# Half products for the last 384 columns of a dense layer, and its activation moved into the next layer

## The chip, the cores and the metric

The program runs on one core of one Trainium2 chip. Its time is device microseconds (us) for one execution; the kernel before is given as the median of 3 executions, and one more execution was recorded by the hardware profiler.

## The reference

```python
x = attention(rmsnorm(q), rmsnorm(k), v)          # 4 batches, 12 heads, 448 tokens, 64 each
x = x.transpose(0, 2, 1, 3).reshape(1792, 768)
# each token goes to one of 8 experts, 224 tokens per expert
out[mask] = np.maximum(x[mask] @ w1[e], 0) @ w2[e]   # w1 768x1024, w2 1024x768
h = out @ w_in                                     # dense layer 1: 768 -> 2048
g = np.where(h > 0, h, np.exp(np.minimum(h, 0)) - 1)   # ELU
return g @ w_out                                   # dense layer 2: 2048 -> 768
```

Inputs and results are float32.

## The kernel before, in words

Every float32 operand of a matmul is split into two float16 tiles (high and low part), and a product takes three matmuls: high x high, high x low, low x high. ScalarE writes the high part, VectorE the low part (`scalar_tensor_tensor`).

Attention and routing come first, then eight experts `e`: `first(e, f)` multiplies into a hidden slice, `second(e, d)` gives 128 of the 768 outputs for the expert's 224 tokens, and `result(e, d, ps)` splits them into `xc`. The tile `xc[0]` holds tokens (columns of the matmul) 0 to 511, `xc[1]` the remaining 384 of a half; the tokens are taken as two rows of 896, index `h`, so that dense layer 1 is a 2x2 block product: input halves of 384 features by token halves of 896 (blocks A), output halves of 1024 by input halves of 384 (blocks B).

Such a 2x2 product can be made of seven half products in place of eight (`winograd`). It needs sums of the operand blocks: S1 = A21+A22, S2 = S1-A11, S3 = A11-A21, S4 = A12-S2, and T1 to T4 in the same way from the weights. In `combine(c, d)` (L964) GpSimd makes S1 to S4 of dense layer 1, for each of the four 128-token chunks `c` of the 512 columns, in three steps `d`; the calls stand between `first` and `second` of experts 2 to 5. `wi_prep(f)` makes weight blocks and T1 to T4 of step `f`: words decoded and split by VectorE and ScalarE.

Dense layer 1 has eight steps `f`, each for two times 128 outputs. In a step, `fewer` (L1173) takes the 512 columns by seven half products of 9 matmuls, and `plain` (L1160) takes the 384 columns by four sums of 18 matmuls, one after each of four half products. Each result goes through `elu` (L1151): Exp and Relu on ScalarE, one `scalar_tensor_tensor` on VectorE, and a store to DRAM `g_d`. Beside it `wi_prep(f + 1)` and `wo_prep(k)`, which prepares layer 2's weights, run on VectorE and ScalarE; the T1 to T4 of layer 2 go to DRAM `t_d`.

Dense layer 2 (L1223 to L1269) has seven groups `g` of two times 128 tokens. `operands(g)` loads the four blocks from `g_d` (tiles `q`), makes their sums on VectorE and splits all seven; `layer2(g, a)` runs seven half products of 24 matmuls of 384 columns into PSUM sums `o_a`, `o_b`, `o_c` and scatters the result. Before group 0, `load_t` (L1100) brings layer 2's T3 and T1 into the tile `ex` (which takes the place of `sums`) and T4 into part of `xc[0]`, 1536 KB each; T2 comes by parts into `t2`.

The order on each engine is the order in the code, apart from the parts where the tile framework places instructions by its own simulated times (the dense layers and `wi_prep`); `issue_after` holds an instruction behind another one. DMAs of these parts are issued by the SP queue.

Of the kernel before, what the change touches and what calls it, by code (L numbers as in the profile page):

```python
# [21 lines left out]
P = 128  # L22
# [761 lines left out]
class Weights:  # L784
# [28 lines left out]
    def fetch(self, pool, w2_d):  # L813

        f = pool.tile([P, 7168], F32, name="b", tag="ex", bufs=1)
# [41 lines left out]
PS = ("a", 2), ("b", 3), ("c", 3)  # L857
A11, A12, S2, S3, S1, S4, A22 = range(7)
# [3 lines left out]
def winograd(pp, name, n, product, snap, add, copy):  # L862

    a, b, c = (pp.tile([P, 512], F32, name=name + t, tag=t, bufs=k)[:, 0:n] for t, k in PS)
    product(b, A11, B11, True)
    p1 = snap(b)
    product(a, A12, B21, True)
    add(a, p1, 0, 0)
    product(b, S2, T2, False)
    u2 = snap(b)  # L870
    product(c, S3, T3, True)
    p7 = snap(c)
    product(b, S1, T1, False)
    add(b, p7, 1, 1)
    product(c, A22, T4, False)
    add(c, u2, 1, 0)
    product(b, S4, B22, False)
    return copy(b, 0, 1)
# [15 lines left out]
def moe(tc, xp, homes, xs, idx, idh, W, rows, ring, w1_d, w2_d, wi_d, wo_d, lin, g_d, t_d, out):  # L894
    nc = tc.nc
    with tc.tile_pool(name="mp", bufs=1, space=PSUM, reuse_waits="tile") as pp:
# [7 lines left out]
        wic, sums, kept = {}, [], []  # L904
# [23 lines left out]
        with tc.tile_pool(name="m1", bufs=1, reuse_waits="tile") as sp:  # L928
# [35 lines left out]
            def combine(c, d):  # L964
                if not sums:
                    x = homes.tile([P, 14336], F16, name="sums", tag="ex", bufs=1)
                    sums.append(x[:, 0:12288].rearrange("p (k d j c) -> p k d j c", k=4, d=3, j=2))
                    kept.extend(x.bitcast(F32)[:, c:c + 512] for c in (6144, 6656))
                x, y = slice(c * P, c * P + P), xc[0]
                s, uv = (z.rearrange("p (k c) -> p k c", k=4) for z in kept)  # L970
                s1, s3, s2, s4 = (s[:, k] for k in range(4))
                u, v = uv[:, 0:2], uv[:, 2:4]
                add = lambda o, p, q, op=ALU.add: nc.gpsimd.tensor_tensor(o, p, q, op)  # L973
                add(u, y[:, 1, d, :, x], y[:, 1, d + 3, :, x])
                add(v, y[:, 0, d, :, x], y[:, 1, d, :, x], ALU.subtract)
                add(s[:, 2:4], y[:, 0, d:d + 4:3, 0, x], y[:, 0, d:d + 4:3, 1, x])
                add(s[:, 0:2], uv[:, 0:4:2], uv[:, 1:4:2])
                add(s2, s1, s2, ALU.subtract)
                add(s4, s4, s2, ALU.subtract)
                hi, lo = (sums[0][:, :, d, j, x] for j in range(2))  # L980
                nc.gpsimd.tensor_copy(hi, s)
                add(lo, s, hi, ALU.subtract)
# [39 lines left out]
            with tc.manual_schedule():  # L1022
# [17 lines left out]
                for e in range(E):  # L1040
# [23 lines left out]
                    for d in range(3 * (1 < e < 6)):  # L1064
                        combine(e - 2, d)
# [9 lines left out]
                    xe[e + 1] = x  # L1075
            wi_prep(0)
            for d in range(6):
                second(E - 1, d, ws[2, E - 1, d])
        with tc.tile_pool(name="wb", bufs=1, reuse_waits="tile") as wp:
# [25 lines left out]
            def operands(g, late=None):  # L1105
# [13 lines left out]
                todo, ahead = [], elus[-1].ins if late else None  # L1119
                held = lambda n: tc.issue_after(ahead) if late and n else ExitStack()  # L1120
                for n, (f, (a11, a12, a21, a22)) in enumerate(parts):
                    s1, s2, s3, s4 = [x[:, f] for x in s]
# [14 lines left out]
                if late:  # L1137
                    for n, k in enumerate((A11, A12, A22, S2)):
                        with held(n > 1):
                            split(k, (ex[:, 12288:14336] if n == 0 else flat[0][:, 2048 * n - 2048:2048 * n]).rearrange("p (f h c) -> p f h c", f=8, h=2))  # L1140
# [7 lines left out]
            elus = []  # L1148

            with tc.tile_pool(name="l1", bufs=1, side="right", reuse_waits="tile") as sp:  # L1150
                def elu(f, cb, k, ps, done=False):  # L1151
                    c0, c1 = CB[cb]
                    h, r = k % 2, k // 2
                    e = sp.tile([P, 512], F32, tag="e", name=f"e{f}_{cb}{h}{r}", bufs=5)[:, 0:c1 - c0]
# [4 lines left out]
                    return e, nc.sync.dma_start(g_d[g, k, :, f].rearrange("g p c -> p g c"), e.rearrange("p (g c) -> p g c", c=P))  # L1159

                def plain(f):
                    n = CB[1][1] - CB[1][0]
                    for h, r in ((0, 0), (0, 1), (1, 0), (1, 1)):
                        t, bufs = PS[2 - r]
                        ps = pp.tile([P, 512], F32, name=f"l{f}_1{h}{r}", tag=t, bufs=bufs)[:, 0:n]
                        w = wic[f + 8 * r]
                        for d in range(6):
                            for m, (i, j) in enumerate(((0, 0), (0, 1), (1, 0))):
                                nc.tensor.matmul(ps, w[:, i, d * P:(d + 1) * P], xc[1][:, h, d, j], start=d == 0 and m == 0, stop=d == 5 and m == 2)  # L1169
                        yield elu(f, 1, 2 * r + h, ps)[1]  # L1170

                def fewer(f, beside):
                    made = {}  # L1173
                    x = {A11: xc[0][:, 0, 0:3], A12: xc[0][:, 0, 3:6], A22: xc[0][:, 1, 3:6]} | dict(zip((S1, S3, S2, S4), (sums[0][:, k] for k in range(4))))
                    w = {B11: (f, 0), B21: (f, 384), B22: (f + 8, 384), T1: ((f, 1), 0), T2: ((f, 1), 384), T3: ((f, 3), 0), T4: ((f, 3), 384)}

                    def product(ps, p, q, first):
                        k, c = w[q]
                        for d in range(3):
                            for m, (i, j) in enumerate(((0, 0), (0, 1), (1, 0))):  # L1180
                                nc.tensor.matmul(ps, wic[k][:, i, c + d * P:c + d * P + P], x[p][:, d, j], start=first and d == 0 and m == 0,  # L1181
                                                 stop=d == 2 and m == 2, skip_group_check=True)
                        if p in (A11, S2, S3, A22):
                            next(beside)

                    homes = [*kept, sp.tile([P, 512], F32, tag="e", name=f"z{f}", bufs=5)]
# [12 lines left out]

                    winograd(pp, f"l{f}_", 512, product, snap, add, copy)  # L1200
                    return made

                for f in range(8):
# [19 lines left out]
            with tc.tile_pool(name="l2a", bufs=1, side="right", reuse_waits="tile") as sa, \  # L1223
# [8 lines left out]
                def layer2(g, a):  # L1232
# [21 lines left out]
                    winograd(pp, f"o{g}_", 384, product, snap, add, copy)  # L1254
# [3 lines left out]
                for g in range(7):  # L1258
                    ops = (first, then, operands(g))[min(g, 2)]
                    if g > 1:  # L1260
                        with tc.issue_after(last.ins):
                            next(ops)
                    elif g:
                        next(ops)
                    else:
                        wt[T4] = load_t(T4, flat[0][:, 6144:12288])
                    behind = lambda k: tc.issue_after(elus[-2].ins if g == 0 else snaps[1 if k in (A11, A12) else 2].ins) if g < 2 else ExitStack()
# [42 lines left out]
```

## Time and profile before

| | |
|---|---|
| median of 3 executions | 942.63 us (940.82 to 944.12) |
| the profiled execution | 941.17 us |
| its span | 939.4 us, mean granted TensorE clock 0.995 |
| PE busy | 918.9 us, 98% of the span |
| DVE busy | 763.2 us, 81% |
| ACT busy | 582.6 us, 62% |
| POOL busy | 370.8 us, 39% |

PE is TensorE's matmuls, PEld its weight loads, DVE VectorE, ACT ScalarE, POOL GpSimd, SP the queue that issues DMAs. The span is what the profiler saw from the first to the last instruction; 941.17 us is the same execution's time, 1.8 us longer. Busy shares are over the whole span, which has stages with different limits: attention and routing to about 290 us, the experts to 540 us, dense layer 1 to 742 us, dense layer 2 to the end. Engine instructions overlap slightly at their ends, so the distance between two starts, not the listed duration, tells what one costs in a busy stretch.

### The profile page before, as it was taken

How to read it: one execution, taken by the hardware profiler on the slowest of the kernel's cores; microseconds unless marked ns; L12 is line 12 of the kernel's file. 1: busy time of each engine (PE TensorE's matmuls, PEld its weight loads, DVE VectorE, ACT ScalarE, POOL GpSimd, SP SyncE). 2: the span in 40 equal slices, each digit the busy share in tenths (PEclk: the TensorE clock that was granted, in tenths of full speed). 3: DMA queues.
4: the chain of work that ended last, by engine and by line, in shares of the span. 5: the costliest groups of instructions: out<-in, count | busy, mean ns of one | idle time of the engine just before them, and what ended most of it. 6: DMA issues, size and time to landing. Idle time of an engine off the chain costs nothing.

```text
span 939.4 us, 18782 instructions
## 1 busy us (share of the span) xinstructions
PE 918.9 (98%) x6855; PEld 614.0 (65%) x6855; DVE 763.2 (81%) x1455; ACT 582.6 (62%) x1251; POOL 370.8 (39%) x552
## 2 busy tenths in 40 slices
PE   7999999999998999999999999999999999999997
PEld 3555555555544899999999955555555566666664
DVE  8999998899868877998888899999999776655430
ACT  7989999999864655566655466666666643333320
POOL 5779999999622200699997000000000001000000
PEclk9999999999998999999999999999999999999999
DMA  9644444453235956887867257777776974232000
GB/s 351 211 111 151 122 141 123 147 165 83 66 83 194 240 185 216 240 228 233 269 218 224 94 187 221 238 226 236 235 230 196 360 265 146 85 105 97 35 35 33
DMA packets 100353, 164.93 MB, mean 176 GB/s; under 512 B 32672, under 2 KB 65952, under 8 KB 99872
## 3 DMA queue, kind: packets, MB, share of 16 engines
q1 hardware_dynamic: 96048, 152.66, 51.9%
q0 software_dynamic: 2400, 11.01, 3.5%
q8 instruction: 55, 0.90, 0.4%
q14 instruction: 42, 0.34, 0.1%
q10 hardware_dynamic: 1808, 0.01, 0.1%
HBM read 131.66 MB, written 31.99 MB: 174 GB/s over the span
## 4 chain that ended last, share of the span: by engine, by line
PE 87%; DVE 6%; POOL 2%; ACT 1%; DMA 1%; issue 1%; POOLq 0%; DVEq 0%; ACTq 0%
PE ph L989 12%; PE py L997 12%; PE o_b L1240 11%; PE l L1169 10%; PE o L320 7%; PE l_b L1181 7%; PE o_c L1240 6%; PE s L243 5%; PE pt L296 4%; PE l_c L1181 3%; PE o_a L1240 3%; PE l_a L1181 2%; DVE s L248 1%; PE xt L948 1%; PE pt L294 1%
## 5 line engine op out<-in xcount | busy, mean ns | idle before, releaser
L1256 POOL DMA_INDIRECT out<-xc,id x14 | 14.6, 1046 | 410.1 <-issue 261.8
L1240 PEld LDWEIGHTS <-a 128*128 128x128 f16 x1080 | 105.7, 98 | 69.8
L1014 DVE SCALAR_TENSOR_TENSOR w<-fw,w 128x768 f16<-128x768 f32 (+1 forms) x90 | 109.3, 1224 | 8.6 <-ACT w L1011 8.4
L997 PE MATMUL py<-h,w 128*128 128x224 f16 x1152 | 114.2, 259 | 0.0
L997 PEld LDWEIGHTS <-w 128*128 128x128 f16 x1152 | 109.8, 98 | 0.2
L248 DVE TENSOR_REDUCE s<-s 128x1 f32<-128x448 f32 x168 | 104.8, 626 | 5.4 <-PE s L243 4.8
L267 ACT ACTIVATE p<-s,nb,r 128x448 f32<-128x448 f32 x144 | 104.4, 726 | 4.1 <-DVE nb L254 3.0
L1169 PE MATMUL l<-xc,wic 128*128 128x384 f16 x576 | 100.3, 326 | 0.0
L989 PE MATMUL ph<-xe,w 128*128 128x224 f16 x1008 | 97.7, 259 | 0.0
L989 PEld LDWEIGHTS <-w 128*128 128x128 f16 x1008 | 96.6, 98 | 0.0
L305 ACT ACTIVATE e<-pt 128x448 f32<-128x448 f32 (+2 forms) x208 | 80.9, 429 | 14.5 <-PE pt L296 14.2
L320 PE MATMUL o<-e,v 128*64 128x448 f32 x384 | 87.8, 558 | 0.0
L1011 ACT ACTIVATE w<-fw 128x768 f16<-128x768 f32 (+1 forms) x90 | 81.7, 921 | 5.7 <-DMA fw<-w 5.7
L1169 PEld LDWEIGHTS <-wic 128*128 128x128 f16 x576 | 56.4, 98 | 41.6
L296 PE MATMUL pt<-idn,p 128*128 128x128 f32 x432 | 70.9, 276 | 0.9 <-ACT p L267 0.9
L296 PEld LDWEIGHTS pt<-idn,p 128*128 128x128 f32 x432 | 50.0, 141 | 23.9 <-ACT e L305 12.3
L1134 DVE SCALAR_TENSOR_TENSOR a<-s,a 128x1024 f16<-128x1024 f32 (+2 forms) x30 | 33.1, 1116 | 33.7 <-ACT a L1133 33.7
L973 POOL TENSOR_TENSOR sums<-sums 128x128 f32<-128x128 f32 (+2 forms) x48 | 58.0, 1208 | 2.8
L243 PE MATMUL s<-ks,qh 128*128 128x448 f16 x144 | 51.2, 355 | 1.9 <-ACT p L267 1.0
L1240 PE MATMUL o_b<-wb,a 128*128 128x384 f16 x312 | 52.0, 326 | 0.0
L243 PE MATMUL s<-ks,ql 128*128 128x448 f16 x144 | 50.7, 352 | 0.0
L961 ACT ACTIVATE xc<-py 128x224 f16<-128x224 f32 (+2 forms) x54 | 18.1, 335 | 51.0 <-PE py L997 46.5
(340 smaller groups left out, 1957.2 us busy)
## 6 DMA issues: line engine op xcount, KB each, us to landing
fw<-w SPq DMA_DIRECT2D x54, 384.0 KB, 3.8
fw<-w SPq DMA_DIRECT2D x36, 512.0 KB, 4.6
xwi<-wi SPq DMA_DIRECT2D x16, 768.0 KB, 7.2
xwo<-wo SPq DMA_DIRECT2D x16, 768.0 KB, 5.1
q<-g_d SPq DMA_DIRECT2D x24, 512.0 KB, 3.7
qT<-qT SPq DMA_DIRECT2D x24, 448.0 KB, 4.2
qk<-qk SPq DMA_DIRECT2D x23, 448.0 KB, 3.5
g_d<-e SPq DMA_DIRECT2D x32, 256.0 KB, 3.7
```

The source lines that it names most:

```text
L243: nc.tensor.matmul(ps[:, 0:448], q[:, o:o + P], ks[:, 448 * h:448 * h + 448], start=n == 0, stop=n == 1)
L248: nc.vector.tensor_reduce(d["s", u][:, 448:449], d["s", u][:, 0:448], AX.X, ALU.max, negate=True)
L267: nc.scalar.activation(dst, d["s", u][:, 0:448], AF.Exp, bias=d["nb", u], scale=d["r"][:, rc:rc + 1], accum_out=d["sm"][:, rc:rc + 1])
L296: nc.tensor.transpose(pt[:, j * P:(j + 1) * P], p[j][:, h, 64 * h + c * P:64 * h + (c + 1) * P], idn)
L320: nc.tensor.matmul(d["o"][64 * h:64 * h + 64, 0:448], d["v"][:, c + 4 * h, :], d["e", min(2 * c + h, 6)], start=c == 0, stop=c == 3)
L989: nc.tensor.matmul(ps, w[:, i, d * P:(d + 1) * P], x[:, d, j], start=d == 0 and n == 0, stop=d == 5 and n == 2)
L997: nc.tensor.matmul(ps, w[:, i, f * P:(f + 1) * P], h[:, f, j], start=f == 0 and n == 0, stop=f == 7 and n == 2)
L1011: nc.scalar.activation(ws[k][:, 0], fs[k], AF.Copy, scale=SW)
L1014: nc.vector.scalar_tensor_tensor(ws[k][:, 1], fs[k], SW, ws[k][:, 0], ALU.mult, ALU.subtract)
L1169: nc.tensor.matmul(ps, w[:, i, d * P:(d + 1) * P], xc[1][:, h, d, j], start=d == 0 and m == 0, stop=d == 5 and m == 2)
L1181: nc.tensor.matmul(ps, wic[k][:, i, c + d * P:c + d * P + P], x[p][:, d, j], start=first and d == 0 and m == 0, stop=d == 2 and m == 2, sk ...
L1240: nc.tensor.matmul(ps, a[x][:, f, i], wt[b][f][:, j], start=first and f == 0 and k == 0, stop=f == 7 and k == 2, skip_group_check=True)
```

## The change

The 384 columns are taken by seven half products as well. The seven products of the two halves alternate (`winograd` is now a generator and yields after each product), with the PSUM tags `b` and `c` exchanged for the third sum. The operand sums of the 384 columns are made by `combine(c)`, c = 4 to 6, and each call now does a whole 128-token chunk in 16 instructions; six of the seven calls run on GpSimd, the last on VectorE. S1 is written over A21 in `xc`; the tile `sums` grows to 19200 float16 and holds the other sums of both halves and a scratch part. Dense layer 1 no longer applies ELU: it scales, adds and stores. ELU is applied in `operands(g)` of layer 2. Layer 2's T3 and T1 now go into parts of the same tile `sums`, T1 behind the last product, and T4 is issued ahead of them.

```diff
+            def combine(c):
...
+                t, eng = c > 3, nc.vector if c == 6 else nc.gpsimd
+                a11, a12, a21, a22 = q = [s[:, k:k + 3] for k in (0, 3, 6, 9)]
+                for k, z in enumerate(q):
+                    add(z, y[:, 3 * k:3 * k + 3, 0, x], y[:, 3 * k:3 * k + 3, 1, x])
+                add(a22, a21, a22)
+                add(a21, a11, a21, ALU.subtract)
+                add(a11, a22, a11, ALU.subtract)
+                add(a12, a12, a11, ALU.subtract)
+                for o, z in zip((y[:, 6:9], sums[t][:, 0:3], sums[t][:, 3:6], sums[t][:, 6:9]), (a22, a11, a12, a21)):
+                    eng.tensor_copy(o[:, :, 0, x], z)
+                    add(o[:, :, 1, x], z, o[:, :, 0, x], ALU.subtract)
...
-                    for d in range(3 * (1 < e < 6)):
-                        combine(e - 2, d)
+                    if e > 1:
+                        combine(e - 2)
...
+            combine(5)
             wi_prep(0)
             for d in range(6):
                 second(E - 1, d, ws[2, E - 1, d])
+            combine(6)
...
+                        for o, z, x in zip(y, t, raw):      # in operands(g)
+                            nc.scalar.activation(z, x, AF.Exp)
+                            nc.scalar.activation(z, z, AF.Relu, bias=1.0, scale=-1.0)
+                            nc.vector.scalar_tensor_tensor(o, x, -1.0, z, ALU.mult, ALU.min)
...
-                    nc.scalar.activation(e, ps, AF.Exp, scale=1.0 if done else CH2)
-                    nc.scalar.activation(e, e, AF.Relu, bias=1.0, scale=-1.0)
-                    elus.append(nc.vector.scalar_tensor_tensor(e, ps, -1.0 if done else -CH2, e, ALU.mult, ALU.min))
+                    return e, nc.scalar.activation(e, ps, AF.Copy, scale=CH2)
...
-                    late = fewer(f, plain(f) if f < 7 else repeat(None))
-                ex = homes.tile([P, 14336], F16, name="ex", tag="ex", bufs=1)
+                    late = {}
+                    both = fewer(f, 0, late), fewer(f, 1, {})
+                    for k in (0, 0, 1, 0, 1, 0, 0, 1, 0, 1, 0, 1, 1, 1) if f == 0 else (0, 1) * 7 if f < 7 else (0,) * 7:
+                        next(both[k])
+                ex = whole[0]
                 first = operands(0, late)
                 next(first)
-                wt = {T3: load_t(T3, ex[:, 0:6144]), T1: load_t(T1, ex[:, 6144:12288])}
+                wt = {T3: load_t(T3, ex[:, 0:6144]), T4: load_t(T4, flat[0][:, 6144:12288])}
                 then = operands(1)
-                for last in plain(7):
-                    next(then)
+                for k, _ in enumerate(both[1]):
+                    if k in (1, 4, 5, 6):
+                        next(then)
+                wt[T1] = load_t(T1, ex[:, 8192:14336])
...
-    nc = bacc.Bacc("TRN2", target_bir_lowering=False, num_devices=1)
+    nc = bacc.Bacc("TRN2", target_bir_lowering=False, num_devices=1, dynamic_dma_scratch_size=8192)
```

The next two pieces are of VectorE where the experts end: `xc_6524<-py_3` to `py_5` are the splits of expert 7's last results, `awi`, `xwi`, `awo`, `xwo` weight words of the two dense layers, `ti` a scratch tile and `wic` split weights of layer 1. First the kernel before:

```order
L962 SCALAR_TENSOR_TENSOR xc_6524<-py_3_10088,xc_6524 128x2x112
L911 SCALAR_TENSOR_TENSOR wic_9992<-awi_9983,wic_9992 128x768
L848 SCALAR_TENSOR_TENSOR awi_10177<-xwi_10178,awi_10177 128x768
L847 SCALAR_TENSOR_TENSOR awi_10183<-xwi_10184,awi_10183 128x768
L920 TENSOR_TENSOR ti_0_9995<-awi_9983,ti_0_9995 128x384
L962 SCALAR_TENSOR_TENSOR xc_6524<-py_4_10115,xc_6524 128x2x112
L846 TENSOR_SCALAR awo_10207<-xwo_10208 128x768
L962 SCALAR_TENSOR_TENSOR xc_6524<-py_5_10142,xc_6524 128x2x112
```

And the same place now:

```order
L973 SCALAR_TENSOR_TENSOR xc_6524<-py_3_10088,xc_6524 128x2x112
L986 TENSOR_TENSOR sums<-xc_6524 128x384 x2
L922 SCALAR_TENSOR_TENSOR wic_9992<-awi_9983,wic_9992 128x768
L848 SCALAR_TENSOR_TENSOR awi_10193<-xwi_10194,awi_10193 128x768
L847 SCALAR_TENSOR_TENSOR awi_10199<-xwi_10200,awi_10199 128x768
L931 TENSOR_TENSOR ti_0_9995<-awi_9983,ti_0_9995 128x384
L973 SCALAR_TENSOR_TENSOR xc_6524<-py_4_10115,xc_6524 128x2x112
L846 TENSOR_SCALAR awo_10223<-xwo_10224 128x768
L973 SCALAR_TENSOR_TENSOR xc_6524<-py_5_10142,xc_6524 128x2x112
```

The first two of the sixteen instructions of `combine(6)` now stand behind `py_3`, ahead of the split of `wic` and of the last two results; the other fourteen follow between the decoding steps after `py_5`.

The next two pieces are of the SP queue at the end of dense layer 1: `xc_6523<-t_d` loads layer 2's T4, `ex<-t_d` T3 and T1, `q<-g_d` the blocks of a group, `g_d<-e` a store of layer 1. First the kernel before:

```order
L1113 DMA q_0_12114<-g_d 128x1024
L1102 DMA xc_6523<-t_d 128x6144
L1159 DMA g_d<-e_011_12017 128x4x128
L1159 DMA g_d<-e_010_12032 128x4x128
L1102 DMA ex<-t_d 128x6144 x2
L1159 DMA g_d<-e_001_12046 128x4x128
```

And the same place now, where `sums<-t_d` are the loads of T3 (the first) and T1 (the last):

```order
L1117 DMA xc_6523<-t_d 128x6144
L1186 DMA g_d<-sums 128x4x128
L1117 DMA sums<-t_d 128x6144
L1186 DMA g_d<-e_001_11843 128x4x128
L1186 DMA g_d<-e_100_11919 128x3x128
L1128 DMA q_2_11933<-g_d 128x1024
L1128 DMA q_1_11934<-g_d 128x1024
L1186 DMA g_d<-sums 128x3x128
L1128 DMA q_3_11935<-g_d 128x1024
L1186 DMA g_d<-e_111_11961 128x3x128
L1117 DMA sums<-t_d 128x6144
```

The loads of T3 and T1, which stood together, are now eight places apart, and T1 stands behind the last store.

## Rows read from the trace of the kernel before

**Rows 1.** Windows: stretch, length, busy time (and instructions) of each engine, clock, DMA.

```profile
541.00:742.00 201.00, 201.00 (x1075) 105.00 (x1074) 195.59 (x302) 127.23 (x215) 0.00 (x0) 1.00 0.73 230
774.00:940.00 166.00, 159.47 (x982) 95.79 (x979) 75.08 (x72) 46.18 (x59) 13.47 (x13) 0.99 0.23 78
```

**Rows 2.** Timeline of PE: start, length, line, operation, out<-in, shape, count.

```profile
512.22 13.96 PE L989 MATMUL ph<-xe,w 128*128 128x224 f16 x144
...
540.25 1.67 PE L1181 MATMUL l_b<-xc,wic 128*128 128x512 f16 x7
...
723.01 2.11 PE L1181 MATMUL l_b<-sums,wic(7, 1)_11725 128*128 128x512 f16 x9
724.95 1.67 PE L1181 MATMUL l_c<-sums,wic(7, 3)_11728 128*128 128x512 f16 x7
...
737.00 5.36 PE L1169 MATMUL l<-xc,wic 128*128 128x384 f16 x32
742.20 2.28 PE L1240 MATMUL o_a<-wb,xc 128*128 128x384 f16 x13
...
750.00 2.11 PE L1240 MATMUL o_c<-ex,a 128*128 128x384 f16 x12
...
757.80 4.06 PE L1240 MATMUL o_b<-ex,a 128*128 128x384 f16 x24
```

**Rows 3.** Timeline of DVE in layer 1, four instructions in a row.

```profile
566.83 0.67 DVE L1157 SCALAR_TENSOR_TENSOR e<-sums,e 128x512 f32<-128x512 f32 x1
567.43 0.94 DVE L847 SCALAR_TENSOR_TENSOR awo<-xwo,awo 128x768 int32<-128x768 int32 x1
568.30 0.54 DVE L1157 SCALAR_TENSOR_TENSOR e<-l,e 128x384 f32<-128x384 f32 x1
568.77 0.67 DVE L1157 SCALAR_TENSOR_TENSOR e<-sums,e 128x512 f32<-128x512 f32 x1
```

**Rows 4.** Lines by form, DVE, 330 to 384 us, then 386 to 510 us.

```profile
L1014 DVE SCALAR_TENSOR_TENSOR w<-fw,w 128x768 f16<-128x768 f32 x13 | 12.2, 950 | 1.9 <-ACT w L1011 1.9
...
L1014 DVE SCALAR_TENSOR_TENSOR w<-fw,w 128x768 f16<-128x768 f32 x37 | 45.2, 1240 | 0.0
```

**Rows 5.** Lines by form, POOL, 384 to 512 us: count, busy us, mean ns.

```profile
L973 POOL TENSOR_TENSOR sums<-xc 128x256 f32<-128x256 f16 x36 | 45.6, 1293 | 0.1
L973 POOL TENSOR_TENSOR sums<-sums 128x128 f32<-128x128 f32 x24 | 22.6, 941 | 1.9
L973 POOL TENSOR_TENSOR sums<-sums 128x512 f16<-128x512 f32 x12 | 21.7, 1812 | 1.0
L973 POOL TENSOR_TENSOR sums<-sums 128x256 f32<-128x256 f32 x12 | 13.7, 1140 | 0.0
L981 POOL CAST sums<-sums 128x512 f16<-128x512 f32 x12 | 12.0, 999 | 0.8
```

**Rows 6.** Timeline of DVE at the gathered rows of expert 7 and at result 3.

```profile
440.99 0.96 DVE L941 TENSOR_TENSOR xh<-xg,xh 112x768 f16<-112x768 f32 x1
...
529.67 0.38 DVE L962 SCALAR_TENSOR_TENSOR xc<-py,xc 128x224 f16<-128x224 f32 x1
```

**Rows 7.** Timeline of SP's queue at the end of layer 1.

```profile
722.99 3.29 SPq L1113 DMA_DIRECT2D q<-g_d  x2
...
735.21 0.32 SPq L1102 DMA_DIRECT2D xc<-t_d  x1
...
738.42 1.73 SPq L1102 DMA_DIRECT2D ex<-t_d  x2
```

**Rows 8.** DMA issues 700 to 800 us: KB each, median us to landing.

```profile
xc<-t_d SPq DMA_DIRECT2D x1, 1536.0 KB, 8.1
```

**Rows 9.** The tile `ex` in the same stretch, its loads.

```profile
DMA to landing us min/median/max: 10.9/12.5/14.0
```

**Rows 10.** Timeline of ACT: the first split of group 0.

```profile
730.03 0.95 ACT L1133 ACTIVATE xc<-q 128x896 f16<-128x896 f32 x1 [2.77 <-DMA q<-g_d]
```

More of the change, by code (lines that the diff above doesn't have):

```diff
@@ L1 @@
-from contextlib import ExitStack
+from contextlib import ExitStack, contextmanager
 from itertools import repeat
@@ L857, with winograd @@
 PS = ("a", 2), ("b", 3), ("c", 3)
+BANKS = (0, 1, 2), (0, 2, 1)
+HOME = 19200
 A11, A12, S2, S3, S1, S4, A22 = range(7)
 B11, B21, B22, T1, T2, T3, T4 = range(7)
-def winograd(pp, name, n, product, snap, add, copy):
-    a, b, c = (pp.tile([P, 512], F32, name=name + t, tag=t, bufs=k)[:, 0:n] for t, k in PS)
+def winograd(pp, name, n, banks, product, snap, add, copy):
+    bank = lambda t, k: pp.tile([P, 512], F32, name=name + "abc"[t], tag=PS[k][0], bufs=PS[k][1])[:, 0:n]
+    a, b = (bank(t, banks[t]) for t in range(2))
     product(b, A11, B11, True)
     p1 = snap(b)
+    yield
     product(a, A12, B21, True)
     add(a, p1, 0, 0)
+    yield
     product(b, S2, T2, False)
     u2 = snap(b)
+    yield
+    c = bank(2, banks[2])
     product(c, S3, T3, True)
     p7 = snap(c)
+    yield
     product(b, S1, T1, False)
     add(b, p7, 1, 1)
+    yield
     product(c, A22, T4, False)
     add(c, u2, 1, 0)
+    yield
     product(b, S4, B22, False)
-    return copy(b, 0, 1)
+    copy(b, 0, 1)
+    yield
 class Rows:
@@ L902, in moe @@
         ix2 = xp.tile([P, 2, E], I32, name="ix2")
-        wic, sums, kept = {}, [], []
+        wic, sums, kept, whole = {}, [], [], {}
         def wi_prep(f):
@@ new lines, in combine @@
+                    x = homes.tile([P, HOME], F16, name="sums", tag="ex", bufs=1)
+                    for a, n in ((0, 512), (9216, 384)):
+                        sums.append(x[:, a:a + 18 * n].rearrange("p (k j c) -> p k j c", k=9, j=2))
+                    scratch, whole[0] = x[:, 16128:19200].bitcast(F32), x
+                    kept.extend((scratch, scratch[:, 0:512], scratch[:, 512:1024], scratch[:, 1024:1408]))
+                t, eng = c > 3, nc.vector if c == 6 else nc.gpsimd
+                x = slice((c - 4 * t) * P, (c - 4 * t) * P + P)
@@ L1118, in operands, with held @@
                     parts.append((slice(7, 8), [late[k][:, 0:P].unsqueeze(1) for k in (0, 2, 1, 3)]))
[L1119 to L1122, printed above, removed]
+                @contextmanager
+                def held(n):
+                    with ExitStack() as x:
+                        for i in ahead if late and n else ():
+                            x.enter_context(tc.issue_after(i))
+                        yield
+                todo, ahead = [], (made[-1].ins, copied[-1].ins) if late else ()
+                for n, (f, raw) in enumerate(parts):
+                    s1, s2, s3, s4 = t = [x[:, f] for x in s]
+                    a11, a12, a21, a22 = y = [x[:, f] for x in q]
                     with held(n):
+                        for o, z, x in zip(y, t, raw):
+                            nc.scalar.activation(z, x, AF.Exp)
+                            nc.scalar.activation(z, z, AF.Relu, bias=1.0, scale=-1.0)
+                            nc.vector.scalar_tensor_tensor(o, x, -1.0, z, ALU.mult, ALU.min)
                         nc.vector.tensor_tensor(s1, a21, a22, ALU.add)
@@ L1146, in operands, with evict @@
                 yield a
-            elus = []
+            made, copied, last = [], [], {}
             with tc.tile_pool(name="l1", bufs=1, side="right", reuse_waits="tile") as sp:
-                def elu(f, cb, k, ps, done=False):
+                def evict(f, cb, k, ps, home=None):
                     c0, c1 = CB[cb]
-                    h, r = k % 2, k // 2
-                    e = sp.tile([P, 512], F32, tag="e", name=f"e{f}_{cb}{h}{r}", bufs=5)[:, 0:c1 - c0]
-                    nc.scalar.activation(e, ps, AF.Exp, scale=1.0 if done else CH2)
-                    nc.scalar.activation(e, e, AF.Relu, bias=1.0, scale=-1.0)
-                    elus.append(nc.vector.scalar_tensor_tensor(e, ps, -1.0 if done else -CH2, e, ALU.mult, ALU.min))
-                    g = slice(c0 // P, c1 // P)
[L1159 to L1174, printed above, removed]
@@ new lines, in evict, with store, fewer @@
+                    e = (kept[home] if f and home else sp.tile([P, 512], F32, tag="e", name=f"e{f}_{cb}{k % 2}{k // 2}", bufs=5))[:, 0:c1 - c0]
+                    return e, nc.scalar.activation(e, ps, AF.Copy, scale=CH2)
+                def store(f, cb, k, e):
+                    c0, c1 = CB[cb]
+                    g = slice(c0 // P, c1 // P)
+                    last[0] = nc.sync.dma_start(g_d[g, k, :, f].rearrange("g p c -> p g c"), e.rearrange("p (g c) -> p g c", c=P))
+                def fewer(f, cb, late):
+                    y, n = xc[cb].rearrange("p h d j c -> p (h d) j c"), CB[cb][1] - CB[cb][0]
+                    x = dict(zip((A11, A12, S1, A22), (y[:, k:k + 3] for k in (0, 3, 6, 9)))) | dict(zip((S2, S4, S3), (sums[cb][:, k:k + 3] for k in (0, 3, 6))))
@@ L1260, in moe @@
                     if g > 1:
-                        with tc.issue_after(last.ins):
+                        with tc.issue_after(last[0].ins):
                             next(ops)
```

53 lines of the change are left out of this document (18 added, 35 removed).

## The prediction, made before the changed kernel was run

> **What bounds the kernel now.** I read the shares by stretch first, then PE's timeline at the edges of the stretches, then the engines beside it. In dense layer 1, 541 to 742 us, PE is busy for 201.00 of 201.00 us and VectorE for 195.59; GpSimd does nothing [rows 1]. The reader should see two full engines: matmuls that go are a gain only if VectorE's work falls as well. In layer 2 (774 to 940) PE has 159.47 of 166 us, VectorE 75.08 and ScalarE 46.18 [rows 1], so there is room beside PE. The clock is 1.00 and 0.99 there, the upper of its two levels.
>
> **PE's matmuls.** Nine of 512 columns take 724.95 - 723.01 = 1.94 us, 0.2157 each; 32 of 384 take 742.20 - 737.00 = 5.20 us, 0.1625 each [rows 2]. A step of layer 1 has 63 x 0.2157 + 72 x 0.1625 = 25.29 us before. Seven half products of nine need 63 of 384 in place of 72: 23.83 us. The order of the changed kernel holds exactly 72 matmuls fewer, so that this is really taken out: 8 x 9 x 0.1625 = **-11.7 us**, if PE stays full.
>
> **VectorE in a step.** From start to start: 0.60 for 512 elements, 0.87 for 768, 0.47 for 384 [rows 3]; the decoding TENSOR_SCALAR of 768 also takes about 0.47, an estimate from its 0.55 us length less the overlap that the others show. `wi_prep` is eight at 0.87 and six at 0.47 (9.78), `wo_prep` seven and seven (9.38), the three additions 1.80, the ELU's last operation 4 x 0.60 + 4 x 0.47 = 4.28: 25.24, beside PE's 25.29. After it the ELU is gone and three additions of 384 come: 9.78 + 9.38 + 1.80 + 1.41 = 22.37, below PE's 23.83. So the steady state follows PE, and VectorE gains on it by 1.5 us a step.
>
> But VectorE starts behind. `combine(6)` puts 16 x 0.47 = 7.5 us into it between expert 7's last results and the first steps, with the split of `wic` and the last two results queued behind its first two instructions. I added the durations in the new order, VectorE from its split of result 3 at 529.67 [rows 6], PE from its first layer-1 matmul at 540.25 [rows 2]. The latest point is the low half of `wic` of step 2: VectorE has 30 of 768, 40 of 384 (or TENSOR_SCALAR), 3 of 512 and six of 224 at about 0.3 ahead of it, 26.1 + 18.8 + 1.8 + 1.8 = 48.5, ready at 578.3; PE has 99 of 512 and 90 of 384, 36.0, and wants it at 576.2. Step 2 is also the one with two `wo_prep`. The later steps are never later than this; step 6 is 2 us early. Stall **+2.0 us**, with 0 (results come a little earlier) and 5 (all of `combine(6)` less the 2.5 that two steps give back) as ends.
>
> **GpSimd and VectorE at once.** The low half of a 768-wide weight takes 950 ns while GpSimd is idle and 1240 while it combines [rows 4], 0.29 more. `combine(5)` runs to about 534 (next paragraph), beside four two-input operations of VectorE after 529.67: 4 x 0.29 = **+1.2**, ends 0 and 2.5 (if those ahead of 529.67 move it as well).
>
> The Trainium skill ("SBUF — State Buffer", section Who interferes with whom) says that a VectorE instruction with two SBUF inputs contends with a GpSimd instruction that reads SBUF, and that the loser blocks for the whole instruction. By that rule the four could each wait for one GpSimd instruction of about 1.5 us, 6.0 in place of 1.2, and the total below would be 942.8. The trace agrees that the two disturb each other, but its mean is 0.29.
>
> **GpSimd's chain.** Twelve steps of the old `combine` took 45.6 + 22.6 + 21.7 + 13.7 + 12.0 = 115.6 us [rows 5], 28.9 for a chunk. A new one has 12 additions of 384 and 4 casts. 384 lies between 256 (1.140; 1.293 from float16) and 512 (1.812): about 1.5, and the casts 0.8 (0.999 for 512) [rows 5]: 21.2. The chain can't start before the gather for expert 7, which follows VectorE's split of 440.99 + 0.96 [rows 6], so `combine(2)` starts near 443.5, and 464.7, 485.9 and 507.1 follow, with `combine(5)` after `first` of expert 7 begins at 512.22 [rows 2] and its data are in: it ends near 534. VectorE reaches `combine(6)`, which shares the scratch part and so waits for GpSimd, at 538.4: 4 us to spare, cost 0. By elements instead (28.9 x 12 x 384 and casts against the old count) a chunk would take 25.1: it ends at 543.9, 5.5 us late, with VectorE's results 4 and 5 and the first `wic` behind.
>
> **The edge of the two layers.** Before, T4 was issued at 735.21 and T3 and T1 together at 738.42 [rows 7]; PE used T3 at 750.00 and T1 at 757.80 without a stop [rows 2]: 11.6 and 19.4 us of cover. After it, T3's place is free only after the last matmul on S4 of the 512 columns in step 7, and PE reaches `o_c` with T3 after 28 matmuls of 384 from there, 4.55 us. T1's place is free after S4 of the 384 columns; PE's first use comes 48 matmuls later, 7.8 us. The nearest rows: T4 (1536 KB) landed in 8.1 us [rows 8], T3 and T1, together in the queue, in 10.9 and 14.0 [rows 9]. T3 is now issued alone but for T4 just ahead, so I take 8.1: stall of T3 8.1 - 4.55 = **+3.6** (10.9: 6.4; lower end 0), of T1 8.1 - 7.8 = **+0.3** (14.0: 6.2; lower end 0). In layer 1 nothing hides these: PE has no other work in its order.
>
> By the Trainium skill ("DMA: Bandwidth & Descriptors", section Anatomy of one DMA, a fit of 2.0 us plus bytes by 436e3, given for GpSimd's path) such a load takes an estimated 5.6 us: T3's stall 1.05, T1's none, and the total 935.2. T4's 8.1 us, beside other loads, speaks against it.
>
> **ELU in front of group 0.** It stood in layer 1; now Exp, Relu and the last operation stand between the last blocks' arrival and the first split. Before, the first load was issued at 722.99 and the first split began at 730.03 [rows 7, 10], 7.0 us. After: eviction 0.5, 7.0, three operations at 0.95 (its length [rows 10]) and the low half 1.1 = 11.5, beside 34 x 0.2157 + 36 x 0.1625 = 13.2 us of PE: 1.7 to spare, cost 0 (ends 0 and 3). In later groups 8 operations of 1024 on ScalarE (0.95 x 1024 / 896 = 1.1) and 4 on VectorE (1.2), 8.8 and 4.9 us, lie beside 7 x 24 x 0.1625 = 27.3 us of PE, where VectorE and ScalarE are half idle or more [rows 1].
>
> **Sum.** -11.7 + 2.0 + 1.2 + 3.6 + 0.3 = -4.6. Against the profiled execution, 941.17 us (span 939.4 and 1.8 around it), that is 936.6. The median of the runs is 1.46 above the profiled one: 938.0.
>
> **Rivals.** A is this forecast. Its own range is 935.5 to 941, the ends being 2.5 off by the two stalls' bounds.
>
> B, both loads land in time, because T3 finds the queues empty and the issue comes earlier than I think: -11.7 + 3.2 = -8.5, 934.1. For it: the change orders T1 last, so that T3 no longer shares with it. Against it: T4 and six stores and loads are near.
>
> C, the other side: T3 and T1 land as slowly as they did [rows 9], since stores of layer 1 and the blocks of group 1 share the DMA engines: stalls 6.4 and 6.2, -11.7 + 3.2 + 12.6 = +4.1, 946.7. Its place is PE's wait before the first matmul on T3 and on T1; it makes the kernel slower as soon as the two stalls exceed 8.5 us together. For it: DMA was busy 73% of layer 1 [rows 1] and 10.9 is measured for exactly this load. Against it: those two were queued one behind the other, 3 MB.
>
> D, GpSimd is slower than I take it: 25.1 a chunk, `combine(5)` ends 5.5 us late and PE starts layer 1 later: 938.0 + 5.5 = 943.5. For it: these instructions are now wider than most that I can measure. Against it: the 512-wide ones took 1.812, not more.
>
> **How the numbers follow.** A 0.47, B 0.25, C 0.15, D 0.13. A measurement of this kernel can tell about 0.3%, 2.8 us: faster is below 939.8, slower above 945.5. Faster: A 0.33, B 0.25, D 0.03 = 0.61. The same: A 0.14, D 0.08, C 0.03 = 0.25. Slower: C 0.12, D 0.02 = 0.14. The range goes from 932 (B with 2 us less stall on VectorE) to 945.5, and leaves out C's upper part and little below.
>
> **What would show it.** Right: 0.1625 us a matmul and 23.8 us a step from step 3 on; gaps of PE of 2 to 3 us in all that wait for VectorE's `wic` in steps 0 to 2; a gap near 3.6 us ahead of the first `o_c` on T3 and hardly one ahead of `o_b` on T1; GpSimd at 21 us a chunk, ending near 534; VectorE not held at `combine(6)`; layer 2's groups without gaps. Wrong: a PE gap ahead of layer 1's first matmul (D), two gaps of 6 us (C) or none (B), gaps of PE that wait for VectorE in steps 3 to 7, or a first group of layer 2 that waits for its splits rather than for a load.

## The result and the profile after

The changed kernel takes 952.72 us (median of 4, 951.39 to 953.73) against 943.38 us for the kernel before on the same chip: ratio 1.0107, 95% interval 1.0084 to 1.0129. Forecast were 938.0 us and a range of 932 to 945.5. The profiled execution took 953.13 us, its span is 951.3 us, 11.9 longer than before.

Read the time between fixed points first. Expert 7's first matmul starts at 528.99 in place of 512.22, and layer 1's main part at 557.02 in place of 540.25 [rows 2]: 16.8 us are lost before layer 1 begins. From there to the end of the products on T3, T4 and T1 it takes 220.55 us in place of 225.52 (765.77 before, 777.57 after): 5.0 are won. The stretch before holds one matmul more, 0.16 us, than the 72 that were taken out; the rest of layer 2 is as long as it was.

TensorE's timeline in the experts of the changed kernel:

```profile
388.43 2.46 PE L1010 MATMUL py<-h,w 128*128 128x224 f16 x24
393.91 0.55 PE L959 MATMUL xt<-idh,xh 112*128 112x112 f16 x8 [3.02 <-DVE xe L963]
394.30 8.72 PE L1010 MATMUL py<-h,w 128*128 128x224 f16 x72
402.86 13.96 PE L1002 MATMUL ph<-xe,w 128*128 128x224 f16 x144
...
436.48 13.96 PE L1002 MATMUL ph<-xe,w 128*128 128x224 f16 x144
...
528.99 13.96 PE L1002 MATMUL ph<-xe,w 128*128 128x224 f16 x144
...
557.02 1.67 PE L1197 MATMUL l_0b<-xc,wic 128*128 128x512 f16 x7
```

The bracket is the idle time ahead of the row and what ended it: PE waits 3.02 us for VectorE's copy of transposed tokens (`xe`), and the 72 matmuls behind it take 8.72 us, where the same row with a full clock has 7.07. The windows around it (length, busy time of PE, PEld, DVE, ACT, POOL, clock):

```profile
390.90:393.90 3.00, 0.00 (x0) 0.00 (x0) 3.00 (x5) 1.09 (x2) 2.90 (x2) 1.00 0.48 129
393.90:397.00 3.10, 3.09 (x24) 2.64 (x24) 3.10 (x5) 0.00 (x0) 2.97 (x3) 0.60 0.54 147
397.00:400.00 3.00, 3.00 (x29) 2.83 (x28) 1.62 (x3) 1.09 (x2) 2.84 (x4) 0.85 0.80 240
```

After the idle stretch the granted clock is 0.60 and 0.85 on average: for a part of it the lower of its two levels. An expert costs 33.62 us from one `first` to the next (402.86 to 436.48) in place of 28.8: 3.0 idle, 0.2 to refill, 1.65 by the clock. This happens at experts 2, 3 and 4, counted from 0 (gaps of 3.02, 3.01 and 3.48): 15.0 of the 16.8 us.

What VectorE and GpSimd do there, from their timelines:

```profile
386.40 4.95 DVE L1027 SCALAR_TENSOR_TENSOR w<-fw,w 128x768 f16<-128x768 f32 x1
...
391.28 1.75 DVE L1027 SCALAR_TENSOR_TENSOR w<-fw,w 128x768 f16<-128x768 f32 x1
```

```profile
385.59 1.41 POOL L901 DMA_INDIRECT xg<-xs,idx  x1 [0.79 <-DMA fw<-w]
387.02 3.50 POOL L986 TENSOR_TENSOR sums<-xc 128x384 f32<-128x384 f16 x4
390.61 1.60 POOL L986 TENSOR_TENSOR sums<-sums 128x384 f32<-128x384 f32 x1
```

A weight split that takes 0.95 us alone [rows 4] takes 4.95. By the trace it starts 0.62 us ahead of the four independent additions that open a `combine`, and ends 0.83 after the last of them; these run at 0.9 us each. At expert 4 it starts only 0.13 ahead and ends 0.83 after them as well. Behind the split stands `xe`, for which PE waits.

In layer 1 and at its end PE waits so (line waited for, us in all, times, longest):

```profile
PE l_1b L1197 <- ACT e L1181: 2.3, 2, 1.7
PE l_0b L1197 <- DVE sums L1207: 1.0, 1, 1.0
PE l_1b L1197 <- DVE sums L986: 0.8, 1, 0.8
PE o_b L1261 <- ACT xc L1266: 0.6, 1, 0.6
PE l_0c L1197 <- DVE e L1207: 0.4, 1, 0.4
PE l_0b L1197 <- ACT e L1181: 0.3, 1, 0.3
```

### The profile page after: what moved, and what is told of

Same layout as the page of the kernel before. It is cut to its first block, busy times and chain, and to the rows that moved or that the text cites. A ratio compares the mean times of both kernels' runs of the same rounds, so it can differ in the third digit from the quotient of the medians.

```text
span 951.3 us, 18577 instructions
## 1 busy us (share of the span) xinstructions
PE 914.6 (96%) x6783; PEld 609.7 (64%) x6783; DVE 792.3 (83%) x1463; ACT 592.0 (62%) x1227; POOL 391.4 (41%) x552
## 4 chain that ended last, share of the span: by engine, by line
PE 71%; DVE 18%; DMA 3%; issue 3%; ACT 2%; POOL 0%; SPq 0%; POOLq 0%; DVEq 0%; ACTq 0%
PE o_b L1261 11%; PE ph L1002 10%; PE py L1010 9%; PE o L320 7%; PE o_c L1261 5%; PE s L243 5%; PE pt L296 5%; PE l_0b L1197 3%; PE l_1b L1197 2%; PE o_a L1261 2%; DVE w L1027 2%; DMA q<-g_d 2%; PE l_0c L1197 1%; PE l_1c L1197 1%; PE s L236 1%
## 5 line engine op out<-in xcount | busy, mean ns | idle before, releaser
L1278 POOL DMA_INDIRECT out<-xc,id x14 | 33.7, 2404 | 366.2 <-ACT xc L1266 239.5
L1027 DVE SCALAR_TENSOR_TENSOR w<-fw,w 128x768 f16<-128x768 f32 (+1 forms) x90 | 122.7, 1375 | 6.3 <-ACT w L1024 6.3
L1010 PE MATMUL py<-h,w 128*128 128x224 f16 x1152 | 119.3, 265 | 0.5 <-DVE h L1004 0.5
L1010 PEld LDWEIGHTS <-w 128*128 128x128 f16 x1152 | 112.9, 100 | 2.8 <-issue 0.6
L1002 PEld LDWEIGHTS <-w 128*128 128x128 f16 x1008 | 96.6, 98 | 0.0
L1197 PEld LDWEIGHTS <-wic 128*128 128x128 f16 x432 | 42.3, 98 | 40.8 <-issue 1.3
L986 POOL TENSOR_TENSOR sums<-sums 128x384 f32<-128x384 f32 (+1 forms) x42 | 62.2, 1481 | 2.9
L901 POOL DMA_INDIRECT xg<-xs,idx x16 | 18.2, 1138 | 102.6 <-DVE xh L952 92.9
```

What stands on the lines that cost most here:

```text
L1002: nc.tensor.matmul(ps, w[:, i, d * P:(d + 1) * P], x[:, d, j], start=d == 0 and n == 0, stop=d == 5 and n == 2)
L1010: nc.tensor.matmul(ps, w[:, i, f * P:(f + 1) * P], h[:, f, j], start=f == 0 and n == 0, stop=f == 7 and n == 2)
L1027: nc.vector.scalar_tensor_tensor(ws[k][:, 1], fs[k], SW, ws[k][:, 0], ALU.mult, ALU.subtract)
```

## The experiments

Three theories stood at the start. P: the four additions behind the gather hold VectorE, PE idles and its clock falls, three times. R: GpSimd's work as a whole slows VectorE. Q: the smaller scratch for DMA descriptors slows the gathers. The kernel before ran beside each set; ratios are to it.

**e1, the sums left out.** `combine(0)` to `combine(5)` are replaced by one memset of the tile:

```diff
+                    nc.gpsimd.memset(x, 0.0)
+                if c < 6:
+                    return
```

> The changed kernel with the GpSimd sums left out: combine(0) to combine(5) only clear the tile once (one memset), combine(6) on VectorE stays; the sums are wrong values. Theory P (a VectorE instruction with two SBUF inputs is held while GpSimd runs the four additions that follow the gather; PE then idles 3 us and runs at half clock for a while, three times): experts take 28.8 us each again, layer 1 starts near 541 in place of 557, 935 to 938 us. Theory R (GpSimd's work as a whole slows VectorE, wherever it stands): the same here, 935 to 938. Theory Q (the smaller DMA scratch of 8192 slows the gathers): within 2 us of 952.7.

936.54 us, ratio 0.9924 (0.9907 to 0.9940), as P and R say. The memset itself, in the same place, holds nobody:

```profile
386.93 16.12 POOL L982 MEMSET sums<- 128x19200 f16 x1
```

**e2, the run split.** The eight additions in another order:

```diff
-                for k, z in enumerate(q):
-                    add(z, y[:, 3 * k:3 * k + 3, 0, x], y[:, 3 * k:3 * k + 3, 1, x])
+                raw = lambda k: add(q[k], y[:, 3 * k:3 * k + 3, 0, x], y[:, 3 * k:3 * k + 3, 1, x])
+                raw(2)
+                raw(3)
                 add(a22, a21, a22)
+                raw(0)
                 add(a21, a11, a21, ALU.subtract)
                 add(a11, a22, a11, ALU.subtract)
+                raw(1)
                 add(a12, a12, a11, ALU.subtract)
```

> The changed kernel with the eight additions of combine in another order: two independent ones, a dependent one, one independent, two dependent, one independent, one dependent; same instructions, same sums. P: the run after the gather is two additions long, VectorE is held 1 to 2 us in place of 4.0, PE's three gaps of 3.0 us go or fall under 1 us and the clock stays up: 938 to 942 us. R and Q: within 2 us of 952.7.

943.22 us, ratio 1.0000 (0.9991 to 1.0010): 9.5 us less than the changed kernel with the same instructions, so R falls. The hold and PE's gaps shrink, less than P had them: the hold is 2.3 us, the gaps are 1.30, 1.30 and 1.77, and the time is 1.2 us above P's range. The 72 matmuls behind the first gap take 7.07 us again. VectorE's split and GpSimd's run:

```profile
385.63 3.23 DVE L1030 SCALAR_TENSOR_TENSOR w<-fw,w 128x768 f16<-128x768 f32 x1
```

```profile
386.25 1.78 POOL L986 TENSOR_TENSOR sums<-xc 128x384 f32<-128x384 f16 x2
```

**e3, the gather moved** behind the four additions of the same `combine`, ahead of the dependent ones.

```diff
+                if between is not None and between < E:
+                    gather(between)
                 add(a22, a21, a22)
```

> The changed kernel with the gather's two DMA_INDIRECT moved behind the four first additions of the same combine call, ahead of the dependent ones. P in its narrow form (VectorE is held only when it already waits while the gather's DMA_INDIRECT runs straight into the four additions): gaps gone, 938 to 943 us. P in its wide form (any run of four back-to-back additions holds VectorE for all four): the hold of 3.5 to 4 us stays, 950 to 953. Q: within 2 us of 952.7. R: within 2 us of 952.7.

940.80 us, ratio 0.9977 (0.9965 to 0.9989). The time is in the range of P's narrow form and the wide form falls, though the gaps shrink rather than go: one addition (1.01 us) now follows the gather straight, the split takes 2.45, the gaps are 0.52, 0.52 and 1.00:

```profile
385.84 2.45 DVE L1029 SCALAR_TENSOR_TENSOR w<-fw,w 128x768 f16<-128x768 f32 x1
```

```profile
386.45 1.01 POOL L986 TENSOR_TENSOR sums<-sums 128x384 f32<-128x384 f32 x1
```

**e4, the scratch alone** in the kernel before (`dynamic_dma_scratch_size=8192`).

> The kernel before with one part of the change alone: dynamic_dma_scratch_size=8192. P and R: 943 us, within 1.5 of the kernel before; the scatters of layer 2 on GpSimd may be longer, off the path. Q: 950 us or more, with PE gaps of 3 us in the experts.

942.27 us, ratio 0.9992 (0.9981 to 1.0004): Q falls.

**e5, combine ahead of the gather.**

```diff
-                    if e + 3 < E:
-                        gather(e + 3)
                     if e > 1:
                         combine(e - 2)
+                    if e + 3 < E:
+                        gather(e + 3)
```

> The changed kernel with GpSimd's order turned: combine(e - 2) stands ahead of gather(e + 3) at each expert, so that nothing of a combine follows a DMA_INDIRECT at once; same instructions. Narrow P (an instruction of VectorE already under way when GpSimd starts a run without a break is held to the run's end, and only the gather brings the two together behind second): PE's three gaps go, 938 to 940 us, at or below the 940.8 of the gather inside. Rival R2 (the run of four holds VectorE wherever a two-input instruction is under way, so that the gaps move to the first matmuls of an expert): 943 to 952.

936.93 us, ratio 0.9940 (0.9926 to 0.9954): a clear gain over both kernels, and as fast as e1, where the sums were left out; R2 falls. The timeline of PE at the place of the first gap:

```profile
388.96 2.46 PE L1010 MATMUL py<-h,w 128*128 128x224 f16 x24
391.26 0.56 PE L959 MATMUL xt<-idh,xh 112*128 112x112 f16 x8
391.66 7.07 PE L1010 MATMUL py<-h,w 128*128 128x224 f16 x72
```

GpSimd's additions still meet VectorE's splits, now in `first`: those of 1024 take 1574 ns on average between 386 and 540 us, 1458 in the changed kernel, and PE doesn't wait for them. One addition of the next `combine` still stands straight behind the gather (396.62, 0.93 us), alone; the weight split beside it takes 1.23 us.

**e6, e9 and e10** ask what the hold needs. The opening four additions become six of 256 (e6) or three of 512 (e9), or two clearings of the scratch, 1.4 us each, stand ahead of them (e10):

```diff
-                for k, z in enumerate(q):
-                    add(z, y[:, 3 * k:3 * k + 3, 0, x], y[:, 3 * k:3 * k + 3, 1, x])
+                for k in range(0, 12, 2):     # e6; in e9 range(0, 12, 4) and k + 4
+                    add(s[:, k:k + 2], y[:, k:k + 2, 0, x], y[:, k:k + 2, 1, x])
```

```diff
+                if c < 6:                     # e10
+                    nc.gpsimd.memset(kept[0], 0.0)
+                    nc.gpsimd.memset(kept[0], 0.0)
```

> The changed kernel with the four additions of 384 that open a combine made as six of 256, back to back, same place behind the gather. P (length of the run decides): VectorE held about 0.7 x 6 = 4 us, PE's gaps stay near 3 us, 951 to 954 us. Rival W (the width of an instruction decides, since the kernel before had three of 256 there without a hold): the hold falls to 1.5 us, gaps go, 938 to 943.

> The changed kernel (gather, then combine) with the four opening additions of 384 made as three of 512, back to back. W (a wide GpSimd instruction holds VectorE's instruction under way to the end of the run, a narrow one of 256 doesn't): VectorE held for 3 x 1.2 = 3.6 us, STT near 5 us, PE's three gaps near 3 us again, 951 to 954. Rival N (what counts is that it is just four, or this shape of three rows): no hold over 2 us, 938 to 943.

> The changed kernel with two clearings of the scratch part (memset, writes only) between the gather and the four additions of each GpSimd combine, so that the run begins about 2.6 us later, when VectorE is past its two splits; all else in place, six combines get 2.6 us longer. U (the hold needs a two-input instruction under way when the run begins): no STT over 2.2 us in experts 4 to 6's second stage, gaps gone or under 1 us, 938 to 944. Rival A (a run of 384-wide additions holds any two-input instruction): a hold of 3 us or more moves to the next split, gaps of 2 to 3 us stay, 948 to 954.

e6 took 942.79 us (one run), without a gap in the experts: what I expected by the run's length is wrong, its rival by width right. e9 took 949.79 (one run), 1.2 us below the range of W, with gaps of 2.87, 2.88 and 3.35, as W says; N falls. e10 took 941.57 (one run): no gap at experts 2 to 4 (the expectation calls them 4 to 6), one of 1.70 us at the end of expert 7. Neither e6 nor e10 gets down to e5's time: PE's gaps from 535 us on come to 10.2 and 8.1 us there, 6.3 in e5. VectorE and GpSimd in e6, then in e9, then in e10:

```profile
385.60 1.50 DVE L1027 SCALAR_TENSOR_TENSOR w<-fw,w 128x768 f16<-128x768 f32 x1
```

```profile
386.21 5.97 POOL L986 TENSOR_TENSOR sums<-xc 128x256 f32<-128x256 f16 x6
```

```profile
385.24 4.81 DVE L1027 SCALAR_TENSOR_TENSOR w<-fw,w 128x768 f16<-128x768 f32 x1
```

```profile
385.84 3.38 POOL L986 TENSOR_TENSOR sums<-xc 128x512 f32<-128x512 f16 x3
```

```profile
389.10 0.94 DVE L1030 SCALAR_TENSOR_TENSOR w<-fw,w 128x768 f16<-128x768 f32 x1
```

```profile
387.95 1.38 POOL L989 MEMSET sums<- 128x1536 f32 x1
389.42 4.72 POOL L986 TENSOR_TENSOR sums<-xc 128x384 f32<-128x384 f16 x4
```

The table sets the length of the run beside that of the split that was under way when it began:

| kernel | additions that open the run | us | split | ends after the run |
|---|---|---|---|---|
| changed | 4 x 384 | 3.50 | 4.95 | 0.83 |
| e9 | 3 x 512 | 3.38 | 4.81 | 0.83 |
| e2 | 2 x 384 | 1.78 | 3.23 | 0.83 |
| e3 | 1 x 384, then a dependent one | 1.01 | 2.45 | 0.83 |
| e6 | 6 x 256 | 5.97 | 1.50 | not held to the end |
| e10 | 4 x 384, behind two memsets | 4.72 | 0.94 | not held |

The last column is the split's start and length less the run's: 386.40 + 4.95 - 387.02 - 3.50 = 0.83. In all rows but e10's the run stands straight behind the gather.

e10's time is the one that U named, but not for U's reason. A split was under way there when the run began (389.10, the run from 389.42), and it was not held: here the first addition waited, 1.40 us in place of 0.91. The same holds in the changed kernel where `combine(3)` follows `combine(2)` and no gather: the split under way at 471.54 takes 1.66 us. So a split under way is not enough; every split that was held to the end of a run met a wide run (384 or 512) straight behind the gather's DMA_INDIRECT. What the gather does to it stays open.

**e7, the last sums left out** (`combine(6)` replaced by a memset on GpSimd, on e5).

```diff
+                if c == 6:
+                    nc.gpsimd.memset(sums[1][:, :, :, x], 0.0)
+                    return
```

> combine_first with the sums of the last chunk left out (combine(6) on VectorE replaced by clearing the slices on GpSimd; these values are wrong). Theory V (VectorE's backlog of 7.5 us at the edge of layer 1 makes the four PE gaps of steps 0 and 1, 2.0 us and their refill): 2 to 3 us less than combine_first. Rival E (these gaps come from evictions on ScalarE and the PSUM banks): within 0.7 us of combine_first.

936.31 us, ratio 0.9935 (0.9921 to 0.9948), 0.6 less than e5; the two intervals overlap. PE's four gaps in steps 0 and 1, 2.0 us in e5, are all gone, as V says, but most of the time was given back in step 7 and at the edge of the layers, at two waits:

```profile
PE o_c L1264 <- DMA sums<-t_d: 2.4, 1, 2.4
PE l_0b L1200 <- ACT sums L1184: 2.1, 1, 2.1
```

**e8, ELU back in layer 1** (on e5): Exp, Relu and `scalar_tensor_tensor` at each result, none in `operands`.

```diff
+                        z = elu(f, cb, 2 * h + r, z, 1.0)[0]      # in add
                         store(f, cb, 2 * h + r, z)
...
-                        z, x = evict(f, cb, 2 * h + r, ps)        # in copy
+                        z, x = elu(f, cb, 2 * h + r, ps, CH2)
```

> combine_first with one part undone: ELU is applied in layer 1 again, at each result of both halves, and layer 2 loads finished blocks. Theory V (VectorE bounds a step: 22.37 + 4.28 = 26.65 us beside PE's 23.83): a step takes 26.6 to 27, layer 1 is 20 to 24 us longer, the edge of the layers 2 to 3 us shorter: 957 to 963 us. Rival (VectorE hides it, since the kernel before was at 25.24 beside 25.29 and fitted): 938 to 943.

969.81 us, ratio 1.0284 (1.0269 to 1.0300): 33 us slower than e5, more than the 20 to 26 expected. VectorE is busy for 174.25 of 180 us and PE only for 157.77, at a mean clock of 0.95, as this window shows:

```profile
560.00:740.00 180.00, 157.77 (x801) 78.83 (x800) 174.25 (x277) 110.92 (x197) 0.00 (x0) 0.95 0.64 201
```

VectorE is full while PE is not, so VectorE bounds a step with ELU in it. PE's longest wait there, 9.4 us, ends with a split of `wic` on ScalarE, which had itself waited 3.5 us for VectorE's decoding. From step 1 to step 7 a step takes 30.3 us on average, where 26.65 was summed; the surplus was not followed up.

**e11 and e12, the edge of the layers** (on e5). e11 exchanges the homes of T3 and T4 and issues two products of the last step earlier; e12 leaves group 0's ELU out.

```diff
-                wt = {T3: load_t(T3, ex[:, 0:6144]), T4: load_t(T4, flat[0][:, 6144:12288])}
+                wt = {T3: load_t(T3, flat[0][:, 6144:12288]), T4: load_t(T4, ex[:, 0:6144])}
...
+                next(both[1])                         # e11, ahead of operands(0, late)
+                next(both[1])
...
+                        for o, z, x in () if late else zip(y, t, raw):     # e12
```

> combine_first with two edits at the edge of the layers: T3 goes to T4's place, which is free earlier, and T4 to T3's; and the first two products of the 384 columns of step 7 are issued ahead of group 0's operands, so that their eviction stands ahead of the late pieces of group 0 on ScalarE. Theory G (the two PE gaps of 1.7 us there come from evictions that stand behind group 0's ELU and splits): the gap ahead of l_1b goes, the one behind the addition of l_0b stays, 1.5 to 2 us less than combine_first's 936.9, 935. Rival: another wait ends last, within 0.8 us of 936.9.

> combine_first without ELU for group 0 of layer 2 (its 128 columns go on without activation; wrong values there), all else as before. G: the two gaps of 1.7 us at the edge shrink to under 0.5 each, 3 us less: 934. Rival D (the load of T3 is close behind and takes the place of the gaps): 936 to 937 with a PE wait of 2 us for T3.

e11: 937.70 us, ratio 0.9956 (0.9940 to 0.9972); e12: 941.99, ratio 0.9997 (0.9987 to 1.0006). The gain that G forecast came in neither: in e11 the 1.7 us ahead of `l_1b` went and 0.6 came ahead of the next product, in e12 1.0 of it was left, and another wait came last. The largest one, in e11 and then in e12:

```profile
PE o_b L1263 <- ACT xc L1268: 2.3, 1, 2.3
```

```profile
PE o_b L1263 <- ACT xc L1268: 3.8, 1, 3.8
```

A result of layer 2 now waits for its eviction on ScalarE. With another set of instructions the framework orders ScalarE's queue anew, so these two runs changed more than they were meant to; which order has no wait at the edge stays open.

## Why the prediction was wrong

**The failed step is "GpSimd and VectorE at once".** I priced it at +1.2 us, as four operations of VectorE beside `combine(5)`, and took experts 2 to 4 as unchanged because the old sums stood there too. Measured: 15.0 us, all at experts 2 to 4, at the place where `combine` follows the gather. My 0.29 us [rows 4] was a mean over the old form, whose additions of 256 let VectorE in between; the new form opens with four of 384 without a break. e1 and e5, where the holds are gone, run at 936.5 and 936.9 us, and the forecast without that term is 936.8; that they meet so closely is partly luck, since the edge's 3.9 us below stood there for another cause. The Trainium skill's rule ("SBUF — State Buffer", section Who interferes with whom), which I weighed against this step, names the right pair of instructions; I applied it at the wrong place. By it the loser waits for one whole instruction; the trace differs, since the split waited for four (e2: two, e9: three), although VectorE had started first.

**Right: PE's matmuls.** From 661.59 to 685.43, the products on S3 in steps 4 and 5, a step takes 23.84 us; 23.83 was forecast.

```profile
661.59 0.59 PE L1197 MATMUL l_0c<-sums,wic(4, 3)_10910 128*128 128x512 f16 x2
...
685.43 2.11 PE L1197 MATMUL l_0c<-sums,wic(5, 3)_11129 128*128 128x512 f16 x9
```

**Right in size and source, not in place: VectorE's backlog.** Gaps of 0.25, 0.39, 0.79 and 0.58, 2.0 us in all, in steps 0 and 1; 2.0 was forecast, for the low half of `wic` in step 2. None waits for `wic`: two wait for VectorE's additions, two for evictions on ScalarE. That `combine(6)` makes them is shown by e7, where it is left out and all four are gone. From 590 to 742 PE has no gap and VectorE is busy for 146.68 of 152 us, where it had 195.59 of 201 [rows 1].

**Right in size, wrong in cause: the edge.** I forecast 3.9 us, for the loads of T3 and T1. The waits there come to 3.3, but PE waited only 0.07 us for T3 and not at all for T1:

```profile
750.91 0.32 SPq L1117 DMA_DIRECT2D sums<-t_d  x1
...
757.32 2.76 PE L1261 MATMUL o_c<-sums,a 128*128 128x384 f16 x16
...
765.35 0.32 SPq L1117 DMA_DIRECT2D sums<-t_d  x1
...
773.67 4.06 PE L1261 MATMUL o_b<-sums,a 128*128 128x384 f16 x24
```

By that short wait T3 landed some 6.4 us after its issue; I had taken 8.1 [rows 8]. The trace of the changed kernel has no landing of these loads. The one of e5 has, for T3, T1 and T4, in this order:

```profile
DMA to landing us min/median/max: 6.7/7.6/8.4
```

The fit in the Trainium skill ("DMA: Bandwidth & Descriptors", section Anatomy of one DMA), given for another path, would be an estimated 5.6; all three took longer, and the trace decides. T3's cover was 6.4 us in place of my 4.55 because a wait that I had at 0 lay in it, the 1.71 us ahead of `l_1b`. The two waits do not add up: without that gap an estimated 6.4 - 4.55 = 1.9 us of T3's would have shown. In e7, where the gap is 0.57 and T3 is used 8.8 us after its issue, PE waits 2.4 us for it. So PE doesn't stop at the loads, as in rival B, but not because the loads are fast.

The time went to 1.04, 1.71 and 0.59 us of waits for evictions and an addition, the first two in the queues behind group 0's ELU, sums and splits, the last behind group 1's ELU. So one of the signs of being wrong came true, "a first group of layer 2 that waits for its splits rather than for a load". The slack of 1.7 us that I gave group 0's ELU was used up; 2.75 us lie within my bound for it, 0 to 3. How much of them is the ELU's own is open: in e12, without it, gaps of 0.54 and 1.02 remain.

```profile
748.73 2.10 PE L1197 MATMUL l_0b<-sums,wic 128*128 128x512 f16 x9 [1.04 <-DVE sums L1207]
...
754.17 1.62 PE L1197 MATMUL l_1b<-sums,wic(7, 1)_11564 128*128 128x384 f16 x9 [1.71 <-ACT e L1181]
```

```profile
751.36 0.30 ACT L1148 ACTIVATE s<-e 128x128 f32<-128x128 f32 x1
751.56 0.50 ACT L1148 ACTIVATE s<-sums 128x128 f32<-128x128 f32 x2
751.96 0.94 ACT L1160 ACTIVATE xc<-q 128x896 f16<-128x896 f32 x1
752.80 0.94 ACT L1160 ACTIVATE xc<-s 128x896 f16<-128x896 f32 x1
753.64 0.48 ACT L1181 ACTIVATE e<-l_1b 128x384 f32<-128x384 f32 x1
```

Seven such gaps cost about 0.17 us of refill each, 1.2 us that no term had: -11.7 + 2.0 + 3.3 + 1.2 = -5.2, beside the measured -5.0, or -4.8 with as many matmuls on both sides.

**GpSimd's chain** (rival D) was no bound: the first four chunks took 17 to 24 us (387.02 to 405.08 the first; 21 forecast), and VectorE was not held at `combine(6)`. Of the 16.8 us, 0.95 were there before expert 2 started, ahead of any sum; expert 0, where they arose, takes 28.8 to 30.2 us over the profiles, the change present or not. And 0.8 came after the third gap, 0.48 of it a wait of PE for VectorE's `h` at 487.12. Neither was followed up.

## What to carry to other kernels

A run of GpSimd instructions without a break can hold a VectorE instruction for the whole run, and everything queued behind it. Here it did so with additions of 384 and 512 straight behind a gather, and not with 256, nor with 384 elsewhere. Ask not only how long GpSimd works, but what stands straight behind one another there and what VectorE has under way at that moment. Before work on a shared resource is made wider, compare its grain with what it was, since a mean per instruction from the old grain does not carry over. Here the cure was the order alone: `combine` ahead of the gather turns 1.0107 into 0.9940.

## What the runs showed that I had not expected

- VectorE's split, though it started first, ends 0.83 us after the run of GpSimd, at four lengths of run, when the run is straight behind the gather. Six additions of 256 in the same place do not hold it so (1.50 us), nor do four of 384 behind a memset (0.94). Why the width and the gather decide was not settled.
- Two waits of PE that lie one behind the other in its order do not add up: with 1.71 us lost ahead of `l_1b`, 0.07 is left for the load of T3, where an estimated 1.9 would have shown without.
- A GpSimd memset of 16.12 us, which only writes, does not slow the splits beside it (two in 1.82 us).
- Idle gaps of 1.3 us left the clock where it was (7.07 us for the 72 matmuls behind); of the six gaps of 2.9 to 3.5 us in the changed kernel and e9 all but one were followed by a stretch at the lower level, which cost 1.65 us each time.
